# The weight pairs of a second MLP get a schedule of their own: staging fetches, sums and splits placed step by step over units 0 to 6

## The chip, the cores and the metric

The kernel runs on one core of one Trainium2 chip. The metric is device time in microseconds (us) of one execution. Five engines appear below: PE (TensorE, matrix products), DVE (VectorE), ACT (ScalarE), POOL (GpSimd) and SP (SyncE, which here only issues transfers). PE, DVE, ACT and SP run their instructions in the order in which the program lists them; an instruction that has to wait holds up everything behind it on its engine.

## The reference

Three stages follow each other. A linear attention over 4 batches, 8 heads, 576 tokens and a head size of 64 gives 2304 tokens of 512 numbers. A mixture of experts sends each token to the best of 8 experts, each with 512 x 1024 and 1024 x 512 weights. A second MLP, the stage of this change, closes:

```
h = x @ w_in            # x: 2304 x 512, w_in: 512 x 2048
g = h * (1.0 / (1.0 + np.exp(-h)))
out = g @ w_out         # w_out: 2048 x 512
```

All of it is in 32-bit floats. The kernel gets nearly that precision from faster products: each operand is split into a rounded high part and the low rest, and three products (high by high, high by low, low by high) are added up in PSUM.

## The kernel before, in words

The part that matters is `x @ w_in`. The 2048 columns of w_in are taken in eight weight pairs of 256 columns (q = 0 to 7), the 2304 tokens in four groups of 576 (k = 0 to 3). One pair with one token group is a unit, u = 8k + q. A unit is a 2 by 2 block product done with seven products instead of eight (a Strassen-Winograd form, numbered 1 to 7), so each weight pair is needed in seven 256-wide combinations of its blocks, and the tokens in seven combinations too. One product is six matmuls of 128 x 288 (`prod`, L1080; `three`, L794). The results go through PSUM banks named puA, puB and puC: ACT copies a finished A bank into a tile ht (`keep`, L1099), and DVE adds a finished B or C bank to such a tile (`join`, L1105); a finished ht tile is stored to the array hd by SP (`hstore`, L1111). There is a ring of 11 ht tiles.

The weight pairs were brought into their form earlier and lie in memory outside the core (sscr). Pairs 0 to 2 were stored with all seven combinations; of pairs 3 to 7 only four blocks were stored, and the other four are summed when they are fetched. For such a pair q the steps are:

- `wfetch(q)` (L975): SP issues one transfer of 0.5 MB from sscr into a staging tile ws. There are two ws buffers, so the fetch of pair q waits until pair q - 2 is done with its staging tile.
- `wsum(q)` (L983): four additions on DVE in the staging tile.
- `whigh(q)` (L991): ACT copies the staging tile, rounded, to the high part of pair q's own tile (wb for pairs up to 3, wbr from 4 on).
- `wlow(q)` (L996): DVE subtracts the high part and leaves the low part there.

Pairs 0 and 1 are split in the stage before. Pair 2 is fetched there, and split here.

`unit` (L1116) lists the work of one unit in the order of products 1, 5, 4, 6, 3, 2, 7, where products 4 and 3 are those of the unit before. Behind each product come its copy or join, and behind these the tasks that the dictionary `todo` holds for (unit, product). `plan` (L1521) fills that dictionary: `at(u, n, task, ...)` hangs a task behind product n of unit u. In all four in-order engines this alone sets the order. Five products of units 0 and 1 are done ahead of unit 0 (EARLYP, L1076), so that unit 0 is short.

Other tasks hang there too. The next token group has to be turned during units 2 to 5: for each of its five token tiles yt, DVE scales the first two (`xscale`, L1014), PE transposes the tile (`xprep`, L1020, four transposes) and ACT copies it out. The scaling of the first tile stands behind product 1 of unit 2, that of the second behind product 1 of unit 3. The last three tiles are gathered by POOL (`xfetch`, L1004) into the two yt buffers. Ahead of unit 7 all engines read a register and branch (L1567 to L1570).

Of the kernel before, what the change touches and what calls it, by code (L numbers as in the profile page):

```python
# [34 lines left out]
NJP = NJ // 2  # L35
# [15 lines left out]
QD = 3  # L51
# [16 lines left out]
def moe_kernel(ctx, tc, qk, v, w_phi, emb, tau, w1, w2, win, wout, out):  # L68
# [185 lines left out]
    def phase_all(ctx):  # L254
# [715 lines left out]
        def wspace(q):  # L970
            wb = (big.tile([P, 2, 2048], F32R, tag="blk", name="wb") if q < 4 else
                  pools["ur"].tile([P, 2, 7 * 256], F32R, tag=f"wb{q}", name="wbr", bufs=1))
            W[q] = (wb[:, 0, 0:7 * 256], wb[:, 1, 0:7 * 256])

        def wfetch(q):  # L975
            if q < QD:
                wspace(q)
                nc.sync.dma_start(out=W[q][1].bitcast(F32), in_=sscr[q].rearrange("p a f -> p (a f)"))
            else:
                W["r", q] = pools["ul"].tile([P, 2048], F32, tag="ws", name="ws", bufs=2)  # L980
                nc.sync.dma_start(out=W["r", q][:, 0:1024], in_=sscr[q].rearrange("p a f -> p (a f)"))
# [528 lines left out]
        slots.close()  # L1510
        pools["ul"] = ctx.enter_context(tc.tile_pool(name="ul", bufs=1, **T))
        pools["ur"] = late.enter_context(tc.tile_pool(name="ur", bufs=1, side="right", **T))
        todo = {}

        def at(u, n, *task):
            todo.setdefault((u, n), []).append(task)

        htile(0, (0, 0))
        for q in range(4, NJP):
            wspace(q)  # L1520
        def plan():  # L1521
            at(0, 6, whigh, 2)
            at(1, 5, wlow, 2)
            for q in range(QD, NJP):
                at(q - 3, 3, wfetch, q)
                at(q - 3, 7, wsum, q)
                at(q - 2, 3, whigh, q)
                at(q - 2, 7, wlow, q)
            for k in range(1, NT // (2 * TN)):
                u = NJP * (k - 1)  # L1530
                for n in range(2 if u else 0):
                    at(u + 1, 1, xfetch, k, n)
                for n, (v, m) in enumerate(((2, 1), (3, 1), (3, 6), (4, 6), (5, 4))):
                    at(u + v, m, xscale, k, n)
                    at(u + v, m, xprep, k, n)
                for n, (v, m) in zip((2, 3, 4), ((2, 5), (3, 5), (4, 1))):
                    at(u + v, m, xfetch, k, n)
                at(u + 4, 2, xsplit, k, "B11")
                at(u + 5, 2, xsum, k, "T1n")
                at(u + 6, 1, xsum, k, "T2n")  # L1540
                at(u + 6, 6, xsum, k, "T3")
                at(u + 6, 2, xsum, k, "T4")
                for v, n, name in ((7, 5, "T1n"), (7, 6, "T2n"), (7, 2, "B21"), (7, 7, "T3"), (8, 4, "T4"), (8, 3, "B22")):
                    at(u + v, n, xsplit, k, name)
            units = [u for u in range(8, 26) if u not in (15, 23)]
            assert len(units) == NJ
            for j, u in enumerate(units):
                at(u - 1, 4, oload, j)
            for j, u in enumerate(units):
                for n in (3, 3, 2, 2):  # L1550
                    at(u, n, cwork, NJ + j)
                at(u, 7, cstore, NJ + j, nc.sync)
            for m in range(4):
                at(26 + m, 1, ofetch, 2 * m)
                at(26 + m, 6, ofetch, 2 * m + 1)
                at(27 + m, 1, ohigh, 2 * m)
                at(27 + m, 5, olow, 2 * m)
                at(27 + m, 6, ohigh, 2 * m + 1)
                at(27 + m, 3, olow, 2 * m + 1)
            at(24, 7, nc.scalar.activation, vec[0:1, 0, 0:1], vec[0:1, 0, 0:1], AF.Silu)  # L1560
            at(25, 1, gload, 0)
            at(30, 3, gate, 0, 0)
            at(31, 3, gate, 0, 1)

        plan()
        for u in range(NUNIT):
            if u == NJP - 1:  # L1567
# [24 lines left out]
    with ExitStack() as c2:  # L1592
        phase_all(c2)
# [31 lines left out]
```

## Time and profile before

| what | value |
|---|---|
| median of 3 runs | 941.25 us (939.53 to 944.82) |
| the profiled execution's own time | 940.23 us |
| its span in the trace | 938.5 us |
| PE busy | 904.0 us, 96% of the span |
| PE weight loads busy | 789.8 us, 84% |
| DVE busy | 624.2 us, 67% |
| ACT busy | 584.5 us, 62% |
| POOL busy | 246.2 us, 26% |

[...] The shares are averages over three stages with different limits; a wait of one stage is hardly seen in them. [...] In the trace's waiting times, "idle before" is the time that the engine stood still ahead of an instruction, and the arrow names what ended it. The issue of a transfer is shown on SP as a row of its own; the transfer itself runs on after it.

### The profile page before, as it was taken

What the parts mean: (1) busy time and instruction counts of PE and PEld (TensorE: products, weight loads), DVE (VectorE), ACT (ScalarE), POOL (GpSimd) and SP (SyncE); (2) the same over time, 40 slices, a digit from 0 to 9 for tenths busy, and PEclk for the clock granted to TensorE, in tenths of its full rate; (3) what the DMA queues carried; (4) which work ended last, traced back from release to release, by engine and by line L of the source; (5) the groups of instructions that cost most, each with busy time, mean ns of one, the idle gap of its engine ahead of it and who ended that gap; (6) DMA issues with size and microseconds to landing.
All of it is one profiled execution on the core that took longest, in us unless ns stands there. A gap on an engine that the chain in (4) does not pass through costs nothing. (4 is left out here: it accounts for less than half of the span.)

```text
span 938.5 us, 15637 instructions
## 1 busy us (share of the span) xinstructions
PE 904.0 (96%) x5567; PEld 789.8 (84%) x5567; DVE 624.2 (67%) x984; ACT 584.5 (62%) x948; POOL 246.2 (26%) x221
## 2 busy tenths in 40 slices
PE   8999999999999999999999678999999999999996
PEld 6999999987677788878888577999999888888885
DVE  7889898886898999979889645676756222222220
ACT  6777887755878889889888434434447344444331
POOL 6877887611201324322100011101000101000000
PEclk9999999999999999999999989999999999999998
DMA  6455353438546728992886333787777844444420
GB/s 178 114 151 165 100 170 93 126 129 323 197 134 233 225 77 234 350 293 57 290 315 227 105 124 122 251 257 235 239 253 241 222 113 112 119 117 112 117 63 22
DMA packets 132114, 164.34 MB, mean 175 GB/s; under 512 B 34424, under 2 KB 93432, under 8 KB 132032
## 3 DMA queue, kind: packets, MB, share of 16 engines
q1 hardware_dynamic: 123296, 141.31, 47.4%
q0 software_dynamic: 8656, 21.96, 8.2%
q8 instruction: 45, 0.74, 0.3%
q14 instruction: 37, 0.30, 0.1%
q10 hardware_dynamic: 80, 0.03, 0.0%
HBM read 165.50 MB, written 46.66 MB: 226 GB/s over the span
## 5 line engine op out<-in xcount | busy, mean ns | idle before, releaser
L845 DVE TENSOR_TENSOR wl<-raw,wh 128x1024 fp32r<-128x1024 f32 (+1 forms) x166 | 188.0, 1174 | 25.2 <-ACT wh L844 19.8
L844 ACT CAST wh<-raw 128x1024 fp32r<-128x1024 f32 (+1 forms) x166 | 162.3, 1024 | 21.8 <-PE ph L797 13.4
L1177 DVE TENSOR_TENSOR hlt<-gt,hlt 128x1024 fp32r<-128x1024 f32 x34 | 41.7, 1226 | 146.4 <-ACT hlt L1176 146.4
L1101 ACT COPY ht<-puA 128x288 f32<-128x288 f32 x128 | 50.8, 400 | 95.2 <-PE puA L797 87.5
L796 PE MATMUL po<-wob,hlt 128*128 128x512 f32 x272 | 108.5, 399 | 0.0
L795 PE MATMUL po<-wob,hlt 128*128 128x512 f32 x272 | 107.2, 394 | 0.0
L797 PE MATMUL po<-wob,hlt 128*128 128x512 f32 x272 | 106.6, 392 | 0.0
L431 POOL TENSOR_TENSOR kl<-ke,kh 128x640 fp32r<-128x640 f32 x52 | 84.1, 1638 | 30.8 <-issue 24.1
L1197 ACT COPY os<-po 128x512 f32<-128x512 f32 x17 | 10.0, 588 | 108.3 <-PE po L797 108.3
L481 PE MATMUL pnx<-kv,qp 128*128 128x73 f32 x640 | 76.6, 275 | 0.0
L481 PEld LDWEIGHTS pnx<-kv,qp 128*128 128x128 f32 x640 | 74.1, 192 | 0.1
L795 PE MATMUL ph<-wh,xh 128*128 128x512 f32 x166 | 67.0, 404 | 0.0
L797 PE MATMUL ph<-wh,xl 128*128 128x512 f32 x166 | 65.1, 392 | 0.8 <-DVE xl L852 0.8
L796 PE MATMUL ph<-wl,xh 128*128 128x512 f32 x166 | 64.8, 390 | 0.0
L1198 POOL DMA_INDIRECT out<-os,oidx x18 | 17.6, 977 | 179.0 <-ACT os L1197 168.6
L392 DVE TENSOR_REDUCE m<-pqk 128x10 f32<-128x1280 f32 x32 | 47.5, 1485 | 24.5 <-PE pqk L386 23.0
L1108 DVE TENSOR_TENSOR ht<-puC,ht 128x288 f32<-128x288 f32 x64 | 29.0, 453 | 51.9 <-PE puC L797 44.4
L795 PEld LDWEIGHTS po<-wob,hlt 128*128 128x128 f32 x272 | 51.1, 188 | 13.1
L1010 POOL DMA_INDIRECT yt<-yd,yidx x13 | 12.9, 991 | 187.3 <-PE pt L1027 160.7
L797 PEld LDWEIGHTS po<-wob,hlt 128*128 128x128 f32 x272 | 51.1, 188 | 12.3
L416 ACT ACTIVATE ke<-d 128x640 f32<-128x640 f32 x52 | 38.3, 737 | 36.9 <-DVE d L393 36.9
L796 PEld LDWEIGHTS po<-wob,hlt 128*128 128x128 f32 x272 | 51.1, 188 | 11.8
(404 smaller groups left out, 2479.2 us busy)
## 6 DMA issues: line engine op xcount, KB each, us to landing
raw<-w SPq DMA_DIRECT2D x44, 1536.0 KB
raw<-w SPq DMA_DIRECT2D x44, 512.0 KB
hd<-ht SPq DMA_DIRECT2D x124, 144.0 KB
gt<-hd SPq DMA_DIRECT2D x15, 1024.0 KB
z<-qk SPq DMA_DIRECT2D x32, 288.0 KB
wo<-wout SPq DMA_DIRECT2D x16, 512.0 KB
yd<-ys SPq DMA_DIRECT2D x23, 256.0 KB
raw<-win SPq DMA_DIRECT2D x10, 512.0 KB
```

Source lines behind the costliest of these rows:

```text
L392: nc.vector.tensor_reduce(out=m, in_=pv, axis=AX.X, op=ALU.max, apply_absolute_value=True)
L416: nc.scalar.activation(out=ke, in_=kd, func=AF.Exp, scale=1.0 - 2.0 * s)
L431: nc.gpsimd.tensor_tensor(out=kl[:, :, s, :], in0=st.pop(("ke", g, s)), in1=kh[:, :, s, :].bitcast(F32), op=ALU.subtract)
L481: nc.tensor.matmul(out=pn[:, c, 0:73], lhsT=qp[:, s, c * P:(c + 1) * P], rhs=kv[:, s, 0:73], start=(s == 0), stop=(s == 1))
L795: nc.tensor.matmul(out=o, lhsT=ah, rhs=bh, start=first, stop=False, skip_group_check=more)
L796: nc.tensor.matmul(out=o, lhsT=ah, rhs=bl, start=False, stop=False, skip_group_check=more)
L797: nc.tensor.matmul(out=o, lhsT=al, rhs=bh, start=False, stop=last, skip_group_check=more)
L844: nc.scalar.copy(out=hi[:, 0:n], in_=sl[:, 0:n])
L845: nc.vector.tensor_tensor(out=lo[:, 0:n], in0=sl[:, 0:n], in1=hi[:, 0:n].bitcast(F32), op=ALU.subtract)
L1101: nc.scalar.copy(out=htile(u, at), in_=BK[u, "A"])
L1108: nc.vector.tensor_tensor(out=o, in0=BK[u, b], in1=o, op=ALU.add)
L1177: nc.vector.tensor_tensor(out=lo, in0=g, in1=hi.bitcast(F32), op=ALU.subtract)
```

## The change

The loop that gave pairs 3 to 7 one regular pattern (fetch at product 3 of unit q - 3, sum at product 7 of the same unit, high part at product 3 and low part at product 7 of unit q - 2) is replaced by a list, one line for each step of each pair. The fetches of pairs 3 and 4 stand ahead of the units altogether. The low part of pair 2 moves from unit 1 to unit 0. From pair 4 on the sum is apart from the fetch by most of a unit or more, and every step of pairs 5 to 7 stands at another place than before.

```
@@ ahead of the units
         pools["ur"] = late.enter_context(tc.tile_pool(name="ur", bufs=1, side="right", **T))
+        wfetch(3)
+        wfetch(4)
         todo = {}
@@ in plan()
             at(0, 6, whigh, 2)
-            at(1, 5, wlow, 2)
-            for q in range(QD, NJP):
-                at(q - 3, 3, wfetch, q)
-                at(q - 3, 7, wsum, q)
-                at(q - 2, 3, whigh, q)
-                at(q - 2, 7, wlow, q)
+            at(0, 3, wlow, 2)
+            at(0, 7, wsum, 3)
+            at(1, 3, whigh, 3)
+            at(1, 7, wlow, 3)
+            at(2, 1, wfetch, 5)
+            at(1, 2, wsum, 4)
+            at(2, 3, whigh, 4)
+            at(2, 7, wlow, 4)
+            at(3, 1, wfetch, 6)
+            at(3, 4, wsum, 5)
+            at(3, 2, whigh, 5)
+            at(4, 1, wlow, 5)
...
+            at(6, 1, whigh, 7)
+            at(6, 4, wlow, 7)
```

The lines left out place pairs 6 and 7: sum of 6 at (4, 3), fetch of 7 at (4, 6), high part of 6 at (5, 1), low part of 6 at (5, 6), sum of 7 at (5, 2).

On DVE, from the end of the stage before to the first scaling of a token tile, the order before is this (L1067 is the last split of the first token group, L1108 a join, L986 the four additions of a pair, L998 a low part, L1018 the scaling of yt):

```order
L1067 TENSOR_TENSOR xcB_6603<-xf,xcB_6603 128x576
L1108 TENSOR_TENSOR ht<-puB,ht 128x288
L986 TENSOR_TENSOR ws<-ws 128x256 x4
L1108 TENSOR_TENSOR ht<-puC,ht 128x288
L998 TENSOR_TENSOR wb<-wb 128x1792
L1108 TENSOR_TENSOR ht<-puC,ht 128x288
L1108 TENSOR_TENSOR ht<-puB,ht 128x288
L998 TENSOR_TENSOR wb<-ws,wb 128x1792
L986 TENSOR_TENSOR ws<-ws 128x256 x4
L1018 TENSOR_SCALAR yt<-yt,gate_s 128x512
```

And with the change:

```order
L1067 TENSOR_TENSOR xcB_6603<-xf,xcB_6603 128x576
L998 TENSOR_TENSOR wb<-wb 128x1792
L1108 TENSOR_TENSOR ht<-puB,ht 128x288
L986 TENSOR_TENSOR ws<-ws 128x256 x4
L1108 TENSOR_TENSOR ht<-puC,ht 128x288 x2
L1108 TENSOR_TENSOR ht<-puB,ht 128x288
L986 TENSOR_TENSOR ws<-ws 128x256 x4
L998 TENSOR_TENSOR wb<-ws,wb 128x1792
L1018 TENSOR_SCALAR yt<-yt,gate_s 128x512
```

The low part of pair 2 has moved ahead of the first join, and the additions of pair 4 ahead of the low part of pair 3; between the additions of pair 4 and the scaling that low part now stands.

On SP, from the last store of the stage before (L933) on, the difference is this (L981 is a staging fetch, sscr_70 to sscr_74 are pairs 3 to 7, L1114 a store of an ht tile):

```order
 L933 DMA yd<-ys 128x512
 L981 DMA ws<-sscr_70 128x1024
-L1114 DMA hd_83<-ht 128x288 x4
 L981 DMA ws<-sscr_71 128x1024
-L1114 DMA hd_83<-ht 128x288 x4
+L1114 DMA hd_83<-ht 128x288 x5
 L981 DMA ws<-sscr_72 128x1024
 L1114 DMA hd_83<-ht 128x288 x4
 L981 DMA ws<-sscr_73 128x1024
-L1114 DMA hd_83<-ht 128x288 x4
+L1114 DMA hd_83<-ht 128x288 x6
 L981 DMA ws<-sscr_74 128x1024
```

The fetch of pair 3 keeps its place, that of pair 4 follows it directly, and the fetches of pairs 5, 6 and 7 have five, nine and fifteen stores of ht tiles ahead of them, where it was eight, twelve and sixteen.

## Rows read from the trace of the kernel before

**Rows 1.** The page: busy tenths of PE in 40 equal slices of the span.

```profile
PE   8999999999999999999999678999999999999996
```

**Rows 2.** Stage view, PE: stretch, its length, PE busy (instructions), granted clock, DMA share, GB/s.

```profile
522.07:592.00 69.93, 52.89 (x361) 0.93 0.42 134
```

**Rows 3.** Waits, 515 to 592: engine, tile, line, releaser: us in total, times, longest.

```profile
PE pt L1027 <- DVE yt L1018: 9.9, 2, 5.3
PE puC L795 <- DVE ht L1108: 4.1, 4, 1.7
PE puA L795 <- PEq L1569: 1.7, 1, 1.7
...
DVE ws L986 <- DMA ws<-sscr: 9.7, 5, 3.5
```

**Rows 4.** Timeline of DVE: start, length, instruction, idle before and its releaser.

```profile
527.32 1.56 DVE L986 TENSOR_TENSOR ws<-ws 128x256 f32<-128x256 f32 x4 [3.54 <-DMA ws<-sscr]
528.80 0.45 DVE L1108 TENSOR_TENSOR ht<-puC,ht 128x288 f32<-128x288 f32 x1
529.16 2.02 DVE L998 TENSOR_TENSOR wb<-wb 128x1792 fp32r<-128x1792 f32 x1
...
536.09 1.55 DVE L986 TENSOR_TENSOR ws<-ws 128x256 f32<-128x256 f32 x4 [2.25 <-DMA ws<-sscr]
537.56 0.48 DVE L1018 TENSOR_SCALAR yt<-yt,gate_s 128x512 f32<-128x512 f32 x1
```

**Rows 5.** Timeline of SP: the issues of the first two staging fetches.

```profile
523.49 0.39 SPq L981 DMA_DIRECT2D ws<-sscr  x1
...
531.93 0.48 SPq L981 DMA_DIRECT2D ws<-sscr  x1
```

**Rows 6.** Timeline of ACT: the rounding of pair 2.

```profile
524.95 1.69 ACT L994 CAST wb<-wb 128x1792 fp32r<-128x1792 f32 x1
```

**Rows 7.** Timeline of PE: first matmuls of products, and transposes.

```profile
529.30 0.40 PE L795 MATMUL puC<-xcB,wb 128*128 128x288 f32 x1 [0.45 <-DVE ht L1108]
...
531.80 0.30 PE L795 MATMUL puA<-xcA,wb 128*128 128x288 f32 x1
...
538.10 1.11 PE L1027 MATMUL pt<-ident,yt 128*128 128x128 f32 x4 [5.34 <-DVE yt L1018]
...
550.31 1.09 PE L1027 MATMUL pt<-ident,yt 128*128 128x128 f32 x4 [4.56 <-DVE yt L1018]
...
555.24 0.60 PE L1027 MATMUL pt<-ident,yt 128*128 128x128 f32 x4
555.60 0.38 PE L795 MATMUL puC<-xcB,wb 128*128 128x288 f32 x1
...
563.56 0.40 PE L795 MATMUL puC<-xcB,wb 128*128 128x288 f32 x1 [1.73 <-DVE ht L1108]
...
579.24 0.30 PE L795 MATMUL puA<-xcT,wbr 128*128 128x288 f32 x1
...
581.93 0.37 PE L795 MATMUL puA<-xcA,wbr 128*128 128x288 f32 x1 [1.74 <-PEq L1569]
...
587.56 0.30 PE L795 MATMUL puA<-xcB,wb 128*128 128x288 f32 x1
```

**Rows 8.** Stage view, PE, columns as in rows 2: stretches around its idle times.

```profile
548.00:548.50 0.50, 0.00 (x0) 0.56 0.11 37
...
538.10:541.20 3.10, 3.10 (x14) 0.50 0.14 50
550.30:554.90 4.60, 4.59 (x20) 0.50 0.32 89
561.70:565.20 3.50, 1.77 (x14) 1.00 0.15 53
```

**Rows 9.** DMA view, 523.4 to 527.4: packets, MB and rate of all queues.

```profile
DMA packets 432, 0.93 MB, mean 234 GB/s; under 512 B 48, under 2 KB 176, under 8 KB 432
```

**Rows 10.** Timeline of POOL, and all transfers into yt: a gather's issue, and times to landing.

```profile
551.67 0.95 POOL L1010 DMA_INDIRECT yt<-yd,yidx  x1 [11.24 <-PE pt L1027]
...
DMA to landing us min/median/max: 3.3/4.6/6.0
```

More of the change, by code (lines that the diff above doesn't have):

```diff
@@ L1522, in plan @@
             at(0, 6, whigh, 2)
-            at(1, 5, wlow, 2)
-            for q in range(QD, NJP):
-                at(q - 3, 3, wfetch, q)
-                at(q - 3, 7, wsum, q)
-                at(q - 2, 3, whigh, q)
-                at(q - 2, 7, wlow, q)
+            at(0, 3, wlow, 2)
[10 more added lines that the diff above has]
+            at(4, 1, wlow, 5)
+            at(4, 6, wfetch, 7)
+            at(4, 3, wsum, 6)
+            at(5, 1, whigh, 6)
+            at(5, 6, wlow, 6)
+            at(5, 2, wsum, 7)
+            at(6, 1, whigh, 7)
+            at(6, 4, wlow, 7)
             for k in range(1, NT // (2 * TN)):
```

## The prediction

> **What bounds the kernel now.** I read the 40 slices of the page first: PE is at 9 almost everywhere, with 6, 7, 8 in the three slices from 516 to 586 us [rows 1]. Behind them it is at 9 to the end, so what PE gains there moves the end one for one. The stage view then sizes the hole: from 522.07 to 592.00 PE is busy 52.89 of 69.93 us at a mean granted clock of 0.93 [rows 2]. That is the start of the second MLP: units 0 to 6, in which the weight pairs 3 to 7 are prepared beside the products.
>
> The list of waits names who holds PE [rows 3]: two waits for the scaling of yt on VectorE (9.9 us), four of product 3 for a join on VectorE (4.1 us), and one at the branch ahead of unit 7 (1.7 us), which no part of the change touches. VectorE in turn waits five times for a staging fetch. Its timeline shows the knot [rows 4]: the sum of pair 4 starts at 536.09, after 2.25 us of waiting for its fetch, and the scaling stands behind it at 537.56; PE's transposes wait until 538.10 [rows 7]. The fetch is so late because its issue, at 531.93, stands behind four stores in SyncE's queue [rows 5]. The same happens a unit later (transposes at 550.31 after 4.56 us idle), and after it in each unit with a join behind the sum (1.73 us at 563.56).
>
> Part of the price is the clock. [...] Half of 3.1 and of 4.5 us is lost, 1.5 and 2.2 us. Around the 1.73 us gap the clock stayed at 1.00 [rows 8].
>
> **The change part by part.** No operation is added or removed: five fetches, twenty adds, six roundings and six subtractions stand in another order. Durations are those of the trace: a subtraction (wlow) 2.02 us, four adds (wsum) 1.56, a join 0.45, a scaling 0.48 [rows 4]; a rounding (whigh) 1.69 [rows 6]. A full-speed unit of seven products takes 587.56 - 581.93 = 5.6 us, 0.80 a product; four transposes take 0.36 (555.24 to 555.60) [rows 7].
>
> *Start, where the change costs.* The low part of pair 2 now precedes unit 0's join on VectorE. It needs whigh 2, done at 524.95 + 1.69 = 526.64 [rows 6], so it runs 526.7 to 528.7; the join ends at 529.05. The adds of pair 3, at 527.32 before [rows 4], start at 529.05 and end at 530.55; the join that they hold up ends at 530.95. Product 3 of unit 0 waits for that join and starts at 531.0 instead of 529.30 [rows 7]: 1.7 us lost. PE is idle about 2.2 us there.
>
> *Fetches 3 and 4 at the head.* Fetch 3 stands where it stood, at 523.49, since the last yd store ahead of it is unchanged; fetch 4 follows at once instead of at 531.93 [rows 5]. Before, the landings took 3.8 and 4.2 us (issue to adds) [rows 4, 5]. In the first 4 us 0.93 MB moved at 234 GB/s [rows 9]; with 0.52 MB more it is 6.2 us. So fetch 3 lands between 527.3, if it is served first, and 529.6, if both are served together, and is wanted at 529.05: a cost of 0 to 0.55 us. I take 0, since transfers of one queue are issued one behind the other. [...]
>
> *First long wait.* From 531.0 three products take the 2.50 us of before (529.30 to 531.80), so unit 2's first product runs 533.5 to 534.3. On VectorE: joins until 533.25, adds of pair 4 until 534.75 with data that landed by 529.6, wlow 3 until 536.75, scaling until 537.15. Transposes at 537.2 instead of 538.10: 0.9 us gained, and PE idle 2.9 us instead of 5.34. What is late next is no longer the fetch but VectorE's own 4.0 us of adds, subtraction and scaling.
>
> *Second long wait.* At full clock six products follow the transposes, then unit 3's first, which ends at 543.2. ScalarE rounds pair 4 once unit 2's product 6 is copied (540.5 to 542.2); wlow 4 until 544.25, scaling until 544.7, transposes at 544.75: idle 1.55 us instead of 4.56. The adds of pair 5 now stand behind the scaling, so the fetch is out of that chain.
>
> *Units 3 to 6.* Fetches 5, 6 and 7 each wait for the low part of the pair two back. They go out at about 536.8, 544.4 and 553.9, land 4.2 us later, and are wanted at 545.0, 555.3 and 562.0: margins of 4.0, 6.7 and 3.9 us. Behind them in SyncE's queue stand only stores of joins that come later on VectorE. The join that product 3 needs no longer has a waiting sum ahead of it, but a whole subtraction (unit 4) or product-side work of 0.75 us; walked through, the smallest slacks are 0 to 1.0 us (unit 5's join; low part of pair 6 before unit 6). The gathers of yt go out 1.4 us after the transposes that free their buffer (550.31, 551.67) and land 4.6 us later, 6.0 at most [rows 7, 10]; the tightest is wanted 8.7 us after, so it holds. I take a cost of 0; if a join of 0.45 us comes late by its own length in each of units 3 to 6, it is 1.8 us.
>
> *Sum.* Before, 538.10 to unit 7's first product at 581.93 is 43.8 us. After: five groups of transposes 1.8, thirty-four products 27.2, the branch gap from 580.04 (579.24 + 0.80) to 581.93, 1.9 [rows 7], the second idle stretch 1.5: 32.4. So 11.4 us there and 0.9 ahead of it, less some 0.1 for restarts: 12.2 us at full clock throughout.
>
> *The clock.* Two new idle stretches lie between what the trace shows: 2.2 and 2.9 us. Up to 1.74 us nothing fell; in the gap of 4.56 us that began at 545.75 the clock had gone down by 548.5 (0.56 in the half microsecond from 548.0 [rows 8]), some 2.3 us into it. A low stretch cost 1.5 or 2.2 us. Bounds: 0 and 4.4 us for both gaps. I take one low stretch of 1.5 us, after the 2.9 us gap, because that gap is longer than those 2.3 us and the other is not. Gain 10.7 us.
>
> The profiled execution took 940.23 us (span 938.5 and 1.7 around it); it becomes 929.5. The median of the runs, 941.25, lies 1.0 above that execution, so I forecast 930.5.
>
> **The rivals.**
> 1. *The clock stays up* (0.25): 12.2 us, 929.0. For it: the short gaps at 1.00; against: the fall 2.3 us into a gap.
> 2. *The clock falls twice* (0.13): 9.2 us, 932.0. For it: the 2.2 and 2.9 us gaps are only 3.3 us apart. Against: the first is as short as the shortest time to a fall.
> 3. *The fetches are late all the same* (0.10): two at once, stores and gathers closer together in a shorter stage. If a landing took 8.4 us, twice 4.2, pair 3 would be 2.9 us late, pairs 5 and 7 0.2 and 0.3: 3.4 us, and two low stretches 3.0: gain 5.8, 935.4. Against: DMA had nothing else to do there, at a mean 134 GB/s [rows 2].
> 4. *Nothing* (0.05): the second staging buffer lies over memory that the stage before still holds, fetch 4 goes out no earlier, and behind it the clock and the later chain eat the rest: within 4.7 us of before. No row shows such a holder behind 523.5.
> 5. *Slower* (0.05): SyncE's in-order queue. Fetches 5 to 7 wait there for a subtraction, and stores of finished ht tiles stand behind them; if the ring of 11 ht tiles ran out, ScalarE's copies would wait for a store, PE for the copies, and the subtraction for PE. Each fetch would then expose its landing and its chain, 4.2 + 1.56 + 1.69 + 2.02 = 9.5 us, three times 28: 28 - 12 gives 957. It decides above 4.1 us per fetch. Against: four tiles a unit and 11 in the ring, and the longest hold that I find is 3.4 us (533.4 to 536.8).
>
> **How the numbers follow.** My forecast has 0.42; with rivals 1 and 2 that is 0.80 between 929.0 and 932.0. 0.5% is 4.7 us, about what a measurement of this kernel can tell from no change. Rival 3 gains 5.8 and counts as faster: faster 0.90, same 0.05, slower 0.05. The range is 927.5 (929.0, and 1.5 for the spread of medians: the runs of before lie 1.7 below to 3.6 above theirs) to 936.5 (rival 3 and 1.1).
>
> **What would show it.** In the profile after: fetch 4 issued within a microsecond of fetch 3; no wait of the adds for a fetch beyond half a microsecond; product 3 of unit 0 at 531.0, 1.7 us later than before; the two waits of the transposes at 2.9 and 1.5 us; no wait of product 3 over 0.3 us in units 4 to 6; unit 7's first product near 571; one stretch at half clock instead of two. I am wrong if the adds still wait for fetches by microseconds, if SyncE's stores are late and ScalarE waits for ht, or if what is gained before 582 is given back behind it.

## The result and the profile after

The changed kernel takes 931.18 us (median of 4 runs, 929.26 to 933.52) against 942.97 us before (4 runs, 939.53 to 944.82): a ratio of 0.988, 95% interval 0.9836 to 0.9924. The forecast was 930.5. The profiled execution of the changed kernel is the slowest of its four, 933.52 us with a span of 931.8; that of before was one of its fastest, 940.23. So the two traces differ by 6.7 us of span and the medians by 11.8, and a part of the work below is to say where the 5 us between these come from.

The page of the kernel after, busy tenths of PE in 40 slices. The hole of [rows 1] (6, 7, 8) has shrunk to 8, 8:

```profile
PE   8999999999999999999999889999999999999996
```

The stage view of the kernel after, over the stretch of [rows 2] (stretch, length, PE busy and instructions, granted clock as a share of full speed, DMA share, GB/s). In the same 69.93 us there are 415 matmuls instead of 361:

```profile
522.07:592.00 69.93, 60.75 (x415) 0.93 0.48 155
```

The waits of PE in the kernel after, 515 to 592 (us in total, times, longest). The transposes wait 3.5 us instead of the 9.9 of [rows 3]; product 3 waits once instead of four times; no engine waits for a staging fetch any more, a line that [rows 3] has with 9.7 us. The wait at the branch has grown from 1.7 to 2.2:

```profile
PE pt L1027 <- DVE yt L1018: 3.5, 2, 2.1
PE puA L795 <- PEq L1585: 2.2, 1, 2.2
PE puC L795 <- DVE ht L1108: 2.1, 1, 2.1
```

The timeline of VectorE in the kernel after (start, length, instruction, idle before and its releaser), to be held against [rows 4]. The low part of pair 2 waits for ScalarE, the join stands behind it, and then the adds of pairs 3 and 4 start without an "idle before" for a transfer:

```profile
527.66 2.02 DVE L998 TENSOR_TENSOR wb<-wb 128x1792 fp32r<-128x1792 f32 x1 [3.50 <-ACT wb L994]
529.60 0.45 DVE L1108 TENSOR_TENSOR ht<-puB,ht 128x288 f32<-128x288 f32 x1
529.97 1.54 DVE L986 TENSOR_TENSOR ws<-ws 128x256 f32<-128x256 f32 x4
...
535.05 1.55 DVE L986 TENSOR_TENSOR ws<-ws 128x256 f32<-128x256 f32 x4
536.52 2.02 DVE L998 TENSOR_TENSOR wb<-ws,wb 128x1792 fp32r<-128x1792 f32 x1
538.46 0.48 DVE L1018 TENSOR_SCALAR yt<-yt,gate_s 128x512 f32<-128x512 f32 x1
```

The timeline of SyncE after: the fetches of pairs 3 and 4 go out as one row of two, 0.97 us together, where [rows 5] has them 8.4 us apart:

```profile
524.48 0.97 SPq L981 DMA_DIRECT2D ws<-sscr  x2
```

The timeline of PE after: unit 1's first product, product 3 of unit 0, the first of unit 2, both waiting transposes, and the first products of units 7 and 8. All of it starts 0.98 us later than before (unit 1's first product was at 522.07), so the comparisons with [rows 7] below count from that product:

```profile
523.05 0.29 PE L795 MATMUL puA<-xcA,wb 128*128 128x288 f32 x1
...
531.94 0.40 PE L795 MATMUL puC<-xcB,wb 128*128 128x288 f32 x1 [2.10 <-DVE ht L1108]
...
538.99 0.66 PE L1027 MATMUL pt<-ident,yt 128*128 128x128 f32 x4 [2.08 <-DVE yt L1018]
...
548.20 0.63 PE L1027 MATMUL pt<-ident,yt 128*128 128x128 f32 x4 [1.44 <-DVE yt L1018]
...
573.96 0.58 PE L795 MATMUL puA<-xcA,wbr 128*128 128x288 f32 x1 [2.24 <-PEq L1585]
...
580.98 0.30 PE L795 MATMUL puA<-xcB,wb 128*128 128x288 f32 x1
```

The stage view of PE after, in three stretches: busy throughout, at half clock (0.54 to 0.55 granted over each, edges included). [rows 8] shows two such stretches before, 3.10 and 4.60 us long at 0.50; here there are three, the last of them behind the branch:

```profile
533.00:536.40 3.40, 3.40 (x17) 0.54 0.43 148
...
539.80:543.30 3.50, 3.50 (x18) 0.55 0.76 250
573.90:577.40 3.50, 3.44 (x15) 0.55 0.18 56
```

From unit 1's first product to unit 8's first, which I call the stage from here on, before took 587.56 - 522.07 = 65.5 us and after 57.9: 7.6 us less. With the 0.98 us of later start that is the 6.7 us of the spans, so behind unit 8 nothing is given back.

### The profile page after: what moved, and what is told of

The parts are those of the page before. It is cut to its first block, busy times and chain, and to the rows that moved or that the text cites. A ratio compares the mean times of both kernels' runs of the same rounds, so it can differ in the third digit from the quotient of the medians.

```text
span 931.8 us, 15638 instructions
## 1 busy us (share of the span) xinstructions
PE 905.0 (97%) x5567; PEld 791.3 (85%) x5567; DVE 624.1 (67%) x984; ACT 583.9 (63%) x948; POOL 245.5 (26%) x221
## 5 line engine op out<-in xcount | busy, mean ns | idle before, releaser
L795 PEld LDWEIGHTS po<-wob,hlt 128*128 128x128 f32 x272 | 51.1, 188 | 13.3
L1108 DVE TENSOR_TENSOR ht<-puC,ht 128x288 f32<-128x288 f32 x64 | 29.0, 453 | 49.7 <-PE puC L797 48.8
L797 PEld LDWEIGHTS po<-wob,hlt 128*128 128x128 f32 x272 | 51.1, 188 | 12.3
L796 PEld LDWEIGHTS po<-wob,hlt 128*128 128x128 f32 x272 | 51.1, 188 | 11.6
L386 PE MATMUL pqk<-wbd,zh 128*128 128x256 f32 (+1 forms) x320 | 59.7, 285 | 0.8 <-DVE d L393 0.6
```

What stands on the lines that cost most here:

```text
L386: nc.tensor.matmul(out=pqk[0:r, c * 256:(c + 1) * 256], lhsT=z[:, c * P:c * P + r], rhs=wbd[:, j].rearrange("p h f -> p (h f)"), start=(i ...
L795: nc.tensor.matmul(out=o, lhsT=ah, rhs=bh, start=first, stop=False, skip_group_check=more)
L796: nc.tensor.matmul(out=o, lhsT=ah, rhs=bl, start=False, stop=False, skip_group_check=more)
L797: nc.tensor.matmul(out=o, lhsT=al, rhs=bh, start=False, stop=last, skip_group_check=more)
```

## The experiments

Each kernel is compared with the kernel before on its own chip. What is concluded rests first on the waits in the traces, one execution each, since the runs of one kernel lie 2 to 8 us apart. In the expectations, which are printed as recorded, "stage" ends earlier than in my text, at unit 7's first product, ahead of unit 7's own time; a table behind the experiments gives both lengths.

**The fetches alone.** Before's places for everything but the fetches (that of pair 7 at (4, 1), where the change has (4, 6)):

```
+        wfetch(3)
+        wfetch(4)
...
-                at(q - 3, 3, wfetch, q)
+                if q > 4:
+                    at(q - 3, 1, wfetch, q)
```

> Only the fetches move (pairs 3 and 4 to the head, pairs 5 to 7 two products earlier); sums, high and low parts stand where they stood before. Stage = from unit 1's first product (522.07 before, 523.05 after) to unit 7's first product (581.93, 573.96): 59.9 us before, 50.9 after. Main theory (the order on VectorE and the clock count beside the fetches): no wait of the adds for a fetch, but the adds still stand ahead of the scaling; waits of the transposes 3.2 and 3.0 us, waits of product 3 of 0.4 and 1.2 us in units 4 and 5; stage 50.0 at full clock, 52 to 53 with one or two low stretches; 8 us faster than before, about 934. Rival (the early fetches are the whole gain): stage as after, 51, and the time of after, 931.

It took 935.76 us (5 runs) against 943.11, ratio 0.9922 (0.9899 to 0.9945): 7.4 us. Its waits of PE in the trace:

```profile
PE pt L1027 <- DVE yt L1018: 5.9, 2, 3.0
PE puC L795 <- DVE ht L1108: 2.1, 4, 0.9
```

Its stage view:

```profile
522.32:582.71 60.39, 49.27 (x328) 0.92 0.45 142
```

The transposes wait 3.0 and 2.9 us, as the walk through VectorE's order had it: the adds no longer wait for a fetch after pair 3's, but they still stand ahead of the scaling. The rival, by which the early fetches are the whole gain, is out by the trace: the stage is 60.4 us where the changed kernel has 57.9, with three low stretches in both. By the times it is out against the changed kernel's second timing below (interval 0.9821 to 0.9863); the interval of the first timing (0.9836 to 0.9924) overlaps.

Here VectorE reached the adds of pair 3 early enough to show when the fetch lands with a second one right behind it. The issue on SyncE, and the adds:

```profile
523.74 0.95 SPq L981 DMA_DIRECT2D ws<-sscr  x2
...
527.85 1.55 DVE L986 TENSOR_TENSOR ws<-ws 128x256 f32<-128x256 f32 x4 [3.81 <-DMA ws<-sscr]
```

That is 4.1 us from issue to adds, and 4.0 and 3.9 in two kernels below (low part back, both parts); the fetch of pair 3 alone took 3.8 to 3.9 in the three executions of before, that of pair 4 4.2 in [rows 4, 5].

**The order alone.** Sums, high and low parts where the change puts them, fetches where they were:

```
-        wfetch(3)
-        wfetch(4)
...
+            for q in range(QD, NJP):
+                at(q - 3, 3, wfetch, q)
```

> Sums, high and low parts stand as after the change, the fetches where they were before. Main theory: the adds of pair 4 wait for their fetch until 536, and now the whole low part of pair 3 stands between them and the scaling: first wait of the transposes 6.5 us instead of 2.1, all later waits as after; stage 51.2 at full clock, 53 to 54 with low stretches; 6 to 7 us faster than before, about 935.5. Rival (the early fetches are the whole gain): the waits for fetches come back in every unit and the time is that of before, 941 to 943.

It took 936.85 us (8 runs) against 943.11, ratio 0.9941 (0.9923 to 0.9958): 6.3 us. The timeline of PE shows the price of the late fetch at the first transposes, and nothing of it at the second:

```profile
542.17 1.12 PE L1027 MATMUL pt<-ident,yt 128*128 128x128 f32 x4 [6.06 <-DVE yt L1018]
...
551.26 0.63 PE L1027 MATMUL pt<-ident,yt 128*128 128x128 f32 x4 [1.44 <-DVE yt L1018]
```

Its stage view:

```profile
522.27:583.07 60.80, 47.22 (x327) 0.92 0.44 133
```

So each half of the change gives about half of the gain (7.4 and 6.3 us, where the whole gave 11.8 and 15.1 in its two timings). The order suffices from unit 3 on: the adds of pair 5 still wait 0.76 us for their fetch there, but behind the scaling, where PE does not wait for them. At pair 4 the early fetch is needed, because its adds have moved ahead of where the old fetch would land: they wait 3.64 us for it.

**The low part of pair 2 back.** In the changed kernel:

```
-            at(0, 3, wlow, 2)
+            at(1, 5, wlow, 2)
```

> As after the change, but the low part of pair 2 back at product 5 of unit 1. Main theory: product 3 of unit 0 waits 0.5 us instead of 2.1; the scaling stays where it was on the clock, less 0.3 to 1.4, since the same work of VectorE stands ahead of it: wait of the transposes 3.2 us; stage 46.2 at full clock, 48 to 49.5 with low stretches; 1 to 2 us faster than after, about 929.5. Rival (the clock alone tells the runs apart): no measurable difference to after, 929 to 933.5.

It took 929.34 us (4 runs) against 943.11, ratio 0.9857 (0.9824 to 0.989). The trace is plain where the runs are not: the join's wait falls from 2.1 to 0.7, and the transposes' first wait rises to 3.0.

```profile
529.11 0.40 PE L795 MATMUL puC<-xcB,wb 128*128 128x288 f32 x1 [0.66 <-DVE ht L1108]
535.57 1.12 PE L1027 MATMUL pt<-ident,yt 128*128 128x128 f32 x4 [3.00 <-DVE yt L1018]
544.59 0.63 PE L1027 MATMUL pt<-ident,yt 128*128 128x128 f32 x4 [1.44 <-DVE yt L1018]
```

```profile
521.67:576.09 54.42, 45.66 (x328) 0.97 0.47 147
```

The stage took 54.4 us, 3.5 less than after's, with one stretch at half clock ahead of unit 7 instead of two and none at the branch, so part of the 3.5 us is the clock. The interval overlaps that of the changed kernel, so that the runs are faster is not shown.

**The scalings early.** In the changed kernel, both scalings at product 5 of unit 0:

```
+            at(0, 5, xscale, 1, 0)
+            at(0, 5, xscale, 1, 1)
...
-                    at(u + v, m, xscale, k, n)
+                    if (k, n) not in ((1, 0), (1, 1)):
+                        at(u + v, m, xscale, k, n)
```

> As after the change, but both scalings of yt stand at product 5 of unit 0, where VectorE waits for ScalarE anyway. Main theory: the transposes wait for nothing any more, the 2.1 us wait of product 3 of unit 0 stays; stage 43.3 at full clock, 44 to 45 with one low stretch; 5 to 7 us faster than after, about 925.5. Rival (VectorE's own adds and subtractions bound these units, and the wait only moves): waits of product 1, for the low part, or of product 3, for the join, of 1 to 3 us in units 2 to 4, and at most 2 us gained, 929.

It took 926.82 us (5 runs) against 943.11, ratio 0.9828 (0.9799 to 0.9858). In its trace both scalings run ahead of unit 1's first product (525.98 here), between the splits of the first token group. There VectorE had stood 0.74 us waiting for ScalarE; its 3.5 us ahead of the low part of pair 2 stay:

```profile
522.64 0.87 DVE L1018 TENSOR_SCALAR yt<-yt,gate_s 128x512 f32<-128x512 f32 x2
...
530.58 2.03 DVE L998 TENSOR_TENSOR wb<-wb 128x1792 fp32r<-128x1792 f32 x1 [3.52 <-ACT wb L994]
```

The waits of the transposes are gone, the join's is unchanged, and the branch takes 2.7:

```profile
PE puA L795 <- PEq L1588: 2.7, 1, 2.7
PE puC L795 <- DVE ht L1108: 2.1, 1, 2.1
```

What held the transposes after the change was thus nothing but the place of a 0.48 us instruction behind VectorE's adds and subtractions; the waits did not move to other products, and only the branch took 0.5 us more. The stage took 53.2 us, with two stretches at half clock:

```profile
525.98:579.15 53.17, 47.05 (x327) 0.94 0.49 157
```

The interval of the ratio overlaps that of the changed kernel, so the runs alone do not show it faster.

**The changed kernel again**, unaltered:

> The changed kernel once more, unaltered. Main theory (the idle stretches of 2.2, 2.9 and 1.5 us and that at the branch lower the clock in some executions and not in others, 1.5 us each): waits in the trace within 0.3 us of the walk at full clock (2.2, 2.9, 1.5) less what a low stretch ahead of them hides; another number of low stretches than the three of the first profile; times spread over 929 to 934, median 930 to 932. Rival (the clock's falls are the same in every execution): again three low stretches at the same places, and a spread as narrow as that of any fixed program, under 1.5 us.

It took 929.41 us (5 runs, 929.07 to 931.44) against 944.46, ratio 0.9842 (0.9821 to 0.9863). The stage view of its PE:

```profile
530.50:533.90 3.40, 3.40 (x16) 0.50 0.41 132
537.30:540.70 3.40, 3.08 (x14) 0.50 0.69 201
540.70:572.40 31.70, 28.07 (x212) 1.00 0.47 147
572.40:578.00 5.60, 5.59 (x42) 1.00 0.44 120
```

Two stretches at half clock instead of three. The first two stand where they stood in the first execution, the one a fraction of a microsecond behind the 2.10 us wait of product 3, the other at the transposes; but the clock did not fall at the branch, though PE waited 2.20 us there against 2.24. The stage is 56.8 us, 1.2 shorter, and the span 2.1: unit 1 starts 1.8 us earlier (521.29), and 0.8 is lost behind unit 8. The median lies 0.6 us below the expected 930 to 932, and the spread of 2.4 us above the rival's 1.5 (no run shows that figure: the kernels timed four times or more spread 2.4 to 7.7 us). So the rival's same three stretches did not come back, and the main theory holds for one of three places only: the falls ahead of unit 7 are the same in both executions.

**PE kept busy.** Needless matmuls in the idle stretches of the changed kernel, their results used nowhere:

```
+        def fill(n):
+            pt = bank("xt", name="fill")
+            for _ in range(n):
+                nc.tensor.matmul(out=pt, lhsT=W[0][0][:, 0:P], rhs=W[0][0][:, 0:512], start=True, stop=True)
...
+            at(1, 6, fill, 8)
+            at(2, 1, fill, 8)
+            at(3, 1, fill, 5)
```

> As after the change, with needless matmuls of 128x512 on PE in the idle stretches: 8 ahead of product 3 in unit 1, 8 ahead of the transposes in unit 2, 5 ahead of those in unit 3 (their results are used nowhere). At full clock one takes 0.23 us, so they fill 1.8, 1.8 and 1.2 of 2.2, 2.9 and 1.5 us. Main theory (low stretches cost 1.5 us each, two of them ahead of the branch): no low stretch between 522 and the branch, the waits for VectorE are left at 0.3 to 1.1 us, stage 47.6 to 48.5, time 1.5 to 3 us below after, about 928.5. Rival (VectorE sets the pace there and the clock costs nothing): the same stage of 51 and the same time as after, 931.

The stage view of this kernel from unit 1's first product to unit 8's, and the transposes in its timeline:

```profile
521.08:575.79 54.71, 49.17 (x349) 1.00 0.48 148
```

```profile
536.33 0.63 PE L1027 MATMUL pt<-ident,yt 128*128 128x128 f32 x4 [1.05 <-DVE yt L1018]
...
543.98 0.63 PE L1027 MATMUL pt<-ident,yt 128*128 128x128 f32 x4 [0.28 <-DVE yt L1018]
```

The clock stays at 1.00, and the stage is 2.0 us shorter than that of the run of the changed kernel beside it (56.8), though the branch took 2.65 instead of 2.20. So in the trace the clock costs 2 us or a little more. In the runs it does not show: 929.24 us (6 runs, 927.35 to 933.43), ratio 0.9848 (0.9825 to 0.9871), where the changed kernel has 929.41; the trace is of the execution that took 927.35. The gain of the filler is not shown by the times.

**Both parts together**: the low part of pair 2 at (1, 5) and both scalings at (0, 5).

> As after the change, with the low part of pair 2 back at product 5 of unit 1 and both scalings at product 5 of unit 0. Main theory (the gains of the two parts add up, since each takes away another wait): waits of 0.5 us for the join in unit 1 and 0.4 in unit 2, none of the transposes, no low stretch ahead of the branch; stage 42.0 to 42.5; 7 us faster than after, 924 to 925. Rival (one wait only covers the other, so that VectorE's load gives back what is taken away): the time of the better of the two parts alone, 926.8.

It took 925.05 us (5 runs, 923.42 to 928.01) against 944.46, ratio 0.9803 (0.978 to 0.9825): the lowest of all, and on the chip of the two kernels above 4.4 us ahead of the changed kernel; each of its five runs lies below each of that kernel's five (929.07 to 931.44). The waits of PE that are left in the stage, and its stage view:

```profile
PE puA L795 <- PEq L1588: 2.2, 1, 2.2
PE puA L795 <- ACT ht L1101: 1.3, 2, 0.8
...
PE puC L795 <- DVE ht L1108: 0.5, 1, 0.5
```

```profile
522.12:570.48 48.36, 44.16 (x327) 1.00 0.52 165
```

The stage is 48.4 us, 17 less than before, at full clock. The time is within 0.1 us of the expected 924 to 925, but the gain on the changed kernel is 4.4 us where 7 were expected, as that kernel took 929.41 here and 931.18 in its first timing. By the times the rival's 926.8 is not excluded. In the trace it is: both waits are gone together, and the stage is shorter than with either part alone (54.4 with one low stretch, 53.2 with two).

**The kernel before, twice more**, with a profile each:

> The kernel before, once more: its runs lie 939.5 to 948.1, its profile at 940.2 was one of the fastest. What the slower ones lose is open. Theory A (the clock): more low stretches than the two of the first profile, at the 1.6 to 1.7 us waits in units 3 to 5 or at the branch, 1.5 us each; stage up to unit 7 of 60 to 63 us. Theory B (the fetches): the adds wait longer for their fetches than the 9.7 us of the first profile, by 2 to 4 us in all. Theory C: the stage is as before, 59.9, and the time is lost ahead of 522 or behind 582.

> As the run ahead of it: a third execution of the kernel before with a profile, to see which of the three (clock, fetches, other stages) goes with its time. If the time is within 1 us of the first profile's 940.2, nothing is told apart.

They took 944.48 and 941.32 us. In the second execution the adds wait 9.7 us for their fetches, as in the first, so theory B falls. That wait, and the stage view of PE, in the 944.48 us execution:

```profile
DVE ws L986 <- DMA ws<-sscr: 9.7, 5, 3.6
```

```profile
537.70:544.50 6.80, 5.20 (x22) 0.50 0.20 60
551.30:558.10 6.80, 5.52 (x24) 0.50 0.24 72
585.30:588.80 3.50, 3.50 (x18) 0.53 0.30 84
```

Theory A holds for the larger part: counted from the first transposes, at 539.30 here, the first low stretch lasts 5.2 us where [rows 8] has 3.1, and there is a third one behind the branch. Its stage is 591.89 - 523.32 = 68.6 us against 65.5, 3.1 of the 4.3 us of span; the other 1.25 us lie ahead of unit 1 (theory C). The third execution, 941.32, was too near the first to tell much: 66.2 us.

The lengths in all the traces: from unit 1's first product to unit 7's, which is the stage of the expectations, and to unit 8's, which is that of my text, in us.

| kernel | unit 1 starts at | to unit 7, expected | to unit 7 | to unit 8 |
|---|---|---|---|---|
| before | 522.07 | | 59.9 | 65.5 |
| before, second and third | 523.32, 522.89 | 60 to 63 (theory A) | 61.4, 60.6 | 68.6, 66.2 |
| changed | 523.05 | | 50.9 | 57.9 |
| changed, again | 521.29 | | 51.1 | 56.8 |
| fetches alone | 522.32 | 52 to 53 | 53.2 | 60.4 |
| order alone | 522.27 | 53 to 54 | 55.2 | 60.8 |
| low part back | 521.67 | 48 to 49.5 | 48.8 | 54.4 |
| scalings early | 525.98 | 44 to 45 | 46.0 | 53.2 |
| PE kept busy | 521.08 | 47.6 to 48.5 | 49.1 | 54.7 |
| both parts | 522.12 | 42.0 to 42.5 | 42.7 | 48.4 |

Five of the expected lengths were missed, by 0.2 to 1.2 us, all on the long side.

## Why the prediction was right, point by point

The waits went as forecast; the clock and the branch were mis-sized, and the time came out as near as it did partly by luck, as the last point says. Counted from unit 1's first product; "filler" is the kernel that kept PE busy, so the walk at full clock can be read from it.

| step | forecast at full clock | after | filler |
|---|---|---|---|
| product 3 of unit 0 (7.23 before) | +1.7 | 8.89: +1.7 | 8.88: +1.7 |
| first transposes (16.03 before) | -0.9 | 15.94: -0.1 | 15.25: -0.8 |
| second transposes (28.24 before) | -5.6 | 25.15: -3.1 | 22.90: -5.3 |
| unit 7's first product (59.86 before) | -12.2 | 50.91: -9.0 | 49.08: -10.8 |

- *The start, where the change costs*: right, 1.66 us against 1.7, with PE idle 2.10 us.
- *Fetches 3 and 4 at the head*: right. The adds of pair 3 started at 529.97, right behind the join, 5.5 us after the fetch went out, so serving both fetches together cost nothing here. The three traces in which VectorE did wait for it show the landing: 3.9 to 4.1 us after the issue, not the 6.2 that I had for two served together. The two issues took 0.97 us on SyncE, where those of [rows 5] took 0.39 and 0.48 each.
- *Both long waits*: right in mechanism. VectorE's adds, subtraction and scaling became the last thing late, as the scaling moved ahead shows, and at full clock both transposes come within 0.3 us of the walk. With the changed kernel's own clock their waits are 2.1 (2.5 in its second trace) and 1.4 where I had 2.9 and 1.5, since PE arrives later, not since VectorE is earlier.
- *Units 3 to 6*: right. The list of waits has product 3 once, in unit 1, and no fetch; ScalarE waited 1.6 us in all for stores of ht tiles, off PE's path, so the rival on the slower side did not come.
- *The branch*: mis-sized. I left it at 1.74; it took 2.24, and 2.2 to 2.7 in every kernel with the new places of sums and splits, against 1.7 to 1.8 in the three of before and in that with the fetches alone. Half a microsecond to one was lost, for a cause that the traces don't show.
- *The clock*: the mis-sized term. I took one low stretch of 1.5 us, half of the 3.10 us that [rows 8] shows at a granted clock of 0.50 (the longer one there, low for some 4.5 of its 4.60 us, gave the 2.2); the first profile has three and the second two. The wait of 2.10 us in unit 1, which I had left at full clock since it is shorter than the 2.3 us after which I saw a fall, was followed by one in both. Ahead of unit 7 two low stretches cost 1.8 us (50.9 against the filler's 49.1, and the filler lost 0.4 more at its branch), the one behind the branch 1.4 (57.93 - 50.91 = 7.0 for a unit that takes 5.6 at full speed). That is rival 2, and in the first profile the branch on top.
- *From the trace to the median*: this made up for it, and that was luck. The trace gained 6.7 us where I had 10.7. Of the missing 4.0, 1.7 were lost up to unit 7, 1.4 behind the branch, and 1.0 ahead of unit 1, where the two kernels run the same instructions; 0.1 came back behind unit 8. The other way, I took the median of before as 1.0 us above its profiled execution; in the result it lies 2.7 above it, and the median of the changed kernel lies 2.3 below its own. So the medians differ by 11.8, and the time came out 0.7 us off the forecast by errors of opposite sign. The traces show two terms in which executions of one kernel differ: the clock (most of the 3.1 us of stage between two executions of before) and the part ahead of unit 1 (1.25 us there, 1.8 between the two of the changed kernel). What the executions without a profile spent where is not known.

## What to carry to other kernels

A wait for a transfer that stands at the head of an in-order engine's queue holds up whatever cheap instruction is queued behind it (in the kernel before, VectorE's adds waited 2.25 us for their fetch with the scaling behind them, and PE was idle for 5.34 [rows 4, 7]), so ask two things apart: can the transfer go out earlier, and can the cheap instruction (here 0.48 us of scaling, whose input was there) go ahead of the wait. Walk the order of both engines through with durations from the trace; that gave the start of the product behind each of the three waits within 0.3 us of a trace at full clock. And look at more than one execution of the kernel before, since a gain worked out from one trace inherits what its clock and its earlier stages happened to do: here 3 us and more than 1.

## What the runs showed of the hardware that was not expected

- The 2.10 us wait of product 3 was followed by half clock in all four traces that have it (the changed kernel twice, the order alone, the scalings early). In the first three the clock fell 0.8, 0.3 and 0.5 us after PE was back at work, in the last at about 534.8, just as PE went on (534.86). The six waits of 1.56 to 1.87 us for joins in units 4 and 5 of the three executions of before were not followed by a fall.
- At the branch the length of the wait does not tell. Behind waits of 1.77 us (the fetches alone), 1.80 (before at 944.48 us), 2.24 (the changed kernel) and 2.70 (the scalings early) PE ran a stretch at half clock; behind waits of 1.74 and 1.76 (before), 2.20 (the changed kernel again, both parts), 2.34 (the low part back), 2.65 (PE kept busy) and 2.67 (the order alone) it did not.
- The branch ahead of unit 7 kept PE idle for 1.74 to 1.80 us in the kernel before and in that with the fetches alone, and for 2.20 to 2.70 us in all others, though PE's own products around it are the same. It stays open why.
